# Pooled attention and a gated product: a fourth seven-product unit in the first product, and another order in the second, from tile 3 on

## The chip, the cores and the metric

The kernel runs on one core of a Trainium2 chip. The metric is the device time in microseconds (us) of one execution, from the first instruction to the last output in memory. The chip's engines work side by side, each through its own list of instructions in order, and wait for each other by semaphores: TensorE (PE) multiplies matrices, into the eight banks of PSUM; VectorE (DVE) and ScalarE (ACT) read PSUM and do element-wise work; GpSimd (POOL) adds and starts transfers; SyncE (SP) starts transfers.

## The reference

```python
# q, k, v: batch 8, 8 heads, 576 rows, 64 wide; float32
k_p = k.reshape(B, H, 72, 8, 64).mean(axis=3)      # 576 rows pooled to 72
v_p = v.reshape(B, H, 72, 8, 64).mean(axis=3)
scores = (1 / sqrt(64)) * q @ k_p^T
attn = softmax(scores)
x = (attn @ v_p) as 4608 tokens x 512

h = x @ w_in                     # 512 x 2048, the "first product"
g = h * sigmoid(h)               # SiLU
out = g @ w_out                  # 2048 x 512, the "second product"
```

The 4608 tokens are worked through in nine tiles of 512 (t = 0 to 8). The attention of batch t + 1 runs in the gaps of tile t, so it lies beside tiles 0 to 6 as a whole batch's work and is absent from tiles 7 and 8.

## The kernel before: the parts concerned

A 2 x 2 block product can be had from seven block products in place of eight, at the price of sums of blocks (Strassen's scheme). The kernel uses it in both products, with the products numbered 1 to 7.

In the first product, one **unit** covers four of the sixteen groups of 128 hidden columns: a block is 256 tokens by 256 hidden columns by 256 of the 512 inputs. The unit has seven products of four matmuls, each 256 columns wide. The sums on the weights (`w_sum1`) are made once, those on x (`x_sum`) once a tile. Three units (A, B, C) cover groups 4 to 15, and groups 0 to 3 are computed plainly, each with four matmuls of 512 columns.

```python
UNITS = ((4, 6), (8, 10), (12, 14))

def product(y, n, bank, first):          # product n of unit y
    ...
    for u in range(2):
        next(step)                       # other work is slipped in by count of steps
        for kk in range(2):
            nc.tensor.matmul(ps[y, bank][:, u, :], lhsT=w[:, kk, 128*u : 128*(u+1)],
                             rhs=x[:, kk, :], start=..., stop=kk == 1)

def stage(y, n):
    if n == "2":   product(y, 2, "P", True);  nc.scalar.copy(r_sb, ps[y, "P"])
    elif n == "5": product(y, 5, "Q", True);  tt(out=rr_sb, in0=ps[y, "Q"], in1=r_sb, op=add)
    elif n == "1": product(y, 1, "R", True);  tt(out=t_sb, in0=ps[y, "R"], in1=rr_sb, op=sub)
    elif n == "4": product(y, 4, "P", False); hidden(y, 1, 0, ps[y, "P"])   # SiLU on ScalarE
    elif n == "3": product(y, 3, "Q", False); hidden(y, 0, 1, ps[y, "Q"])
    elif n == "7": product(y, 7, "P", False); tt(out=c_sb[0], in0=ps[y, "P"], in1=t_sb, op=add)
    elif n == "6": product(y, 6, "Q", False); tt(out=c_sb[1], in0=ps[y, "Q"], in1=t_sb, op=add)
    elif n == "h": hidden(y, 0, 0, c_sb[0])
    else:          hidden(y, 1, 1, c_sb[1])

def plain(t, step, g, n0, n):            # one group without the scheme
    for kk in range(4): nc.tensor.matmul(hp_ps[...], lhsT=w_in_sb[:, kk, g*128:(g+1)*128],
                                         rhs=xT[:, kk, ...])        # 512 columns
    nc.scalar.activation(h_T[:, g, ...], hp_ps, func=AF.Silu)
```

P and Q of the units rotate through five PSUM buffers tagged "at", which the attention's tiles use too; R, the plain groups and the three banks of the second product rotate through three tagged "mm". `r_sb`, `rr_sb`, `t_sb` and the two `c_sb` exist once.

In the second product a tile is one such block product, with seven products of sixteen matmuls, 256 columns wide. Its left sides are sums of hidden values (`h_sum`, bf16 operations on VectorE), except for products 3 and 4, which read the plain hidden values `h_T`:

```python
def down_quarters(t, fillers, last=False):
    product(2, KA, KQ); product(5, KA, KQ); product(2, 0, KA)
    nc.scalar.copy(r_sb, ps["P"])
    product(5, 0, KA)
    tt(out=rr_sb, in0=ps["Q"], in1=r_sb, op=add)
    for cc in ((0,), (1,)) if last else ((0, 1),):
        product(1, ...);  tt(out=t_sb, in0=ps["R"], in1=rr_sb, op=sub)
        product(4, ...);  nc.scalar.copy(o_sb[1][:, cs, LO], ps["P"])
        product(3, ...);  nc.vector.tensor_copy(out=o_sb[0][:, cs, HI], in_=ps["Q"])
        product(7, ...);  tt(out=o_sb[0][:, cs, LO], in0=ps["P"], in1=t_sb, op=add); store(...)
        product(6, ...);  tt(out=o_sb[1][:, cs, HI], in0=ps["Q"], in1=t_sb, op=add); store(...)
```

The attention of the next batch and the sums are slipped in between the matmuls at counted steps:

```python
f_down.append((33, lambda: hidden_sum(7, 0, 8)))
...
sc_at, den_at, nu_at = (1, 31, 75), (31, 56, 97), (56, 97, 101)   # scores, denominators, numerators
...
for n in (4, 1, 3, 7, 6):
    f_down.append((98 if t < B - 1 else 44, lambda n=n: unit_x_sum(t + 1, n)))
```

Of the kernel before, what the change touches and what calls it, by code (L numbers as in the profile page):

```python
# [27 lines left out]
FP32 = mybir.dt.float32  # L28
# [8 lines left out]
def kernel(  # L37
# [9 lines left out]
    nc = tc.nc  # L47
# [43 lines left out]
    def ps_tile(shape, dtype, tag, name):  # L91
        return psum.tile(shape, dtype, tag=tag, bufs=banks[tag], name=name)
# [24 lines left out]
            singles.tile([128, 5, 2, 256], BF16, name=f"w_sum1{n}") for n in range(2)  # L117
        )
    ]
    x_sum = singles.tile([128, 5, 2, NQ], BF16, name="x_sum")  # L120
    gate = singles.tile([128, 1], BF16, name="gate")
    c_sb = [singles.tile([128, 2, NQ], FP32, name=f"c_sb{n}") for n in range(2)]
# [54 lines left out]
    def load_one(b, name):  # L177
        st = batches.setdefault(b, {})
        raw = raw_tile(f"{name}_raw", H)
        nc.gpsimd.dma_start(out=raw, in_=source(b, name)[:, :, :PH])  # L180
        st[f"{name}_raw"] = raw
# [10 lines left out]
        )  # L192
        nc.gpsimd.tensor_add(out=dst, in0=raw[:, :, :D], in1=raw[:, :, D : 2 * D])

    def behind_x_sums():
        nc.gpsimd.tensor_copy(out=gate[:1], in_=x_sum[:1, U_XI[6], 0, :1])  # L196

    def pool_k(b):
        pool_rows(kp[:SP], batches[b]["k_raw"])
# [119 lines left out]
    def third(n):  # L319
        return tuple((g, n * QV, (n + 1) * QV) for g in range(2))  # L320
# [78 lines left out]
    def attn_tables():  # L399
        nc.scalar.preload_act_table_set("natural_log_exp_and_others")  # L400
# [13 lines left out]

    UNITS = ((4, 6), (8, 10), (12, 14))
    UW = [
        {
            (i, j): w_in_sb[:, 2 * j : 2 * j + 2, 128 * u : 128 * (u + 2)]  # L420
# [14 lines left out]
    def unit_weight_sum(y, n):  # L435
        a, b = U_W[n]
        nc.vector.tensor_tensor(
            out=w_sum1[y][U_WI[n]], in0=UW[y][a], in1=UW[y][b],
            op=ALU.subtract if n in (6, 7) else ALU.add,
        )  # L440
# [19 lines left out]
    def up(t, fillers, items):  # L460
        step = spread(
            fillers,
            sum(
                KF if len(it) == 3 else 2 * len(it[1].strip("hs")) for it in items
            ),
        )
        ps = {}

        def product(y, n, bank, first):
            if first:  # L470
                tag = "mm" if bank == "R" else "at"
                ps[y, bank] = ps_tile([128, 2, NQ], FP32, tag, f"u_ps{bank}")
            w, x = unit_weights(y, n), unit_x(t, n)
            for u in range(2):
                next(step)
                for kk in range(2):
                    nc.tensor.matmul(  # L477
                        ps[y, bank][:, u, :], lhsT=w[:, kk, 128 * u : 128 * (u + 1)],
                        rhs=x[:, kk, :], start=first and u == 0 and kk == 0,
                        stop=kk == 1, skip_group_check=True,  # L480
                    )

        def hidden(y, i, j, src):
            g = UNITS[y][i]
            nc.scalar.activation(  # L485
                h_T[:, g : g + 2, j * NQ : (j + 1) * NQ], src, func=AF.Silu
            )

        tt = nc.vector.tensor_tensor

        def stage(y, n):
            if n == "2":
                product(y, 2, "P", True)
                nc.scalar.copy(r_sb, ps[y, "P"])  # L494
            elif n == "5":
                product(y, 5, "Q", True)
                tt(out=rr_sb, in0=ps[y, "Q"], in1=r_sb, op=ALU.add)  # L497
            elif n == "1":
                product(y, 1, "R", True)
                tt(out=t_sb, in0=ps[y, "R"], in1=rr_sb, op=ALU.subtract)  # L500
            elif n == "4":
                product(y, 4, "P", False)
                hidden(y, 1, 0, ps[y, "P"])
            elif n == "3":
                product(y, 3, "Q", False)
                hidden(y, 0, 1, ps[y, "Q"])
            elif n == "7":
                product(y, 7, "P", False)
                tt(out=c_sb[0], in0=ps[y, "P"], in1=t_sb, op=ALU.add)  # L509
            elif n == "6":  # L510
                product(y, 6, "Q", False)
                tt(out=c_sb[1], in0=ps[y, "Q"], in1=t_sb, op=ALU.add)  # L512
            elif n == "h":
                hidden(y, 0, 0, c_sb[0])
            else:
                hidden(y, 1, 1, c_sb[1])

        for it in items:
            if len(it) == 3:
                plain(t, step, *it)  # L520
            else:
                for n in it[1]:
                    stage(it[0], n)
        for _ in step:
            pass

    def plain(t, step, g, n0, n):
        tag = "at" if (t, g, n0) == (0, 3, 0) else "mm"
        hp_ps = ps_tile([128, 512], FP32, tag, "hp_ps")
        c0 = (t * NTT + n0) % NX  # L530

        for r0, r1 in ((0, min(n, NX - c0)), (min(n, NX - c0), n)):
            for kk in range(KF) if r1 > r0 else ():
                if r0 == 0:
                    next(step)
                x0 = (c0 + r0) % NX
                nc.tensor.matmul(  # L537
                    hp_ps[:, r0:r1],
                    lhsT=w_in_sb[:, kk, g * 128 : (g + 1) * 128],
                    rhs=xT[:, kk, x0 : x0 + r1 - r0],  # L540
                    start=(kk == 0), stop=(kk == KF - 1),
                )
        nc.scalar.activation(h_T[:, g, n0 : n0 + n], hp_ps[:, :n], func=AF.Silu)  # L543
# [58 lines left out]
    def hidden_sum(n, k0, k1):  # L602
        a, b, op = H_SUMS[n]
        ks = slice(k0, k1)
        nc.vector.tensor_tensor(  # L605
            out=h_sum[n][:, ks, :], in0=quarter(*a, ks), in1=quarter(*b, ks), op=op
        )
# [17 lines left out]
    def left(n, kt, c):  # L625
        cs = slice(128 * c, 128 * (c + 1))
        if n in h_sum:
            return h_sum[n][:, kt, cs]
        i = n - 3
        return h_T[:, i * KQ + kt, i * NQ + 128 * c : i * NQ + 128 * (c + 1)]  # L630
# [55 lines left out]
            pass  # L686


    warm_ps = ps_tile([128, 512], FP32, "mm", "warm_ps")

    def warm_up(n):
# [97 lines left out]
        " C6 Ch Cs g2 g3",  # L789
    )  # L790
    visits = [third(n) for n in range(3)]
    for t in range(NT):
        a = t + 1
        f_up, f_down = [], []
        if t == 0:
            GA = 11
            items = [(g, 0, HS) for g in range(GA)]
            items += [(g, HS, NTT - HS) for g in range(GA)]
            items += [(g, 0, NTT) for g in range(GA, KG)]
            f_up += [(1, lambda: denominators(0, part(0, 1), on_dve=True))]  # L800
            f_up += [(5, lambda: denominators(0, part(1, 1), on_dve=True))]
            f_up += [(13, lambda: numerators(0, part(0, 1)))]
            f_up += [(17, lambda: numerators(0, part(1, 1)))]
        else:
            G = lambda *gs: [(g, 0, NTT) for g in gs]
            if t == 1:
                items = (
                    G(12, 13, 14, 15) + [(0, "25143"), (1, "2"), (0, "7"), (1, "5")]
                    + [(0, "6h"), (1, "1")] + G(0) + [(1, "4"), (0, "s"), (1, "3")] + G(1)
                    + [(1, "7h6")] + G(2) + [(1, "s")] + G(3)  # L810
                )
            else:
                items = []
                for it in THREE[t // B].split():
                    items += [(("BCA".index(it[0])), it[1])] if it[0] in "ABC" else G(int(it[1]))
            if t == 1:
                for n in U_X:
                    f_up.append((0, lambda n=n: unit_x_sum(t, n)))
            for n in (2, 5):
                h_at = 50 if t == B else 54 if t > 1 else 45  # L820
                f_up.append((h_at, lambda n=n: hidden_sum(n, 4, 8)))
            f_up.append((56, lambda: hidden_sum(6, 4, 8)))
            for n, k0 in ((2, 0), (5, 0), (1, 4), (1, 0)):
                f_up.append((64, lambda n=n, k0=k0: hidden_sum(n, k0, k0 + 4)))
            f_down.append((33, lambda: hidden_sum(7, 0, 8)))
            f_down.append((71 if t < B else 50, lambda: hidden_sum(6, 0, 4)))

        for n, t0, f_to, at, parts in (
# [71 lines left out]
        if t == 1:  # L900
            def unit_weight_tiles():
                k_w = big.tile([128, 4, 2, 256], BF16, tag="k_raw2", name="w_sum12")
                v_w = big.tile([128, 4, 2, 256], BF16, tag="v_raw2", name="w_sum12")
                w_sum1.append([k_w[:, i] for i in range(4)] + [v_w[:, 0]])

            f_down.append((72, unit_weight_tiles))
            for i, n in enumerate(U_W):
                f_down.append((73 if i < 2 else 81, lambda n=n: unit_weight_sum(2, n)))
        if t != 1:
            moe_tables()  # L910
        if t == 0:
# [34 lines left out]
```

The softmax here doesn't subtract the row's maximum and nothing guards it: scores larger than these inputs give would overflow.

## Time and profile before

| | |
|---|---|
| time, median of three | 280.02 us (279.89 to 280.05) |
| span of the profiled execution | 278.3 us |
| granted TensorE clock | 1.000 |
| tile 1 (50.8 to 81.0) | 30 us |
| tiles 2, 3, 4, 5, with a batch's attention | 28.7 us each |
| tile 6, with one visit of numerators more | 29.3 us |
| tile 7, without attention | 24.9 us |

The busy share of an engine is the time in which it executed anything, over the span. Matmuls are pipelined, so a busy TensorE can still hold small waits; the sum of its pieces, from the chain of waits, shows whether it does. The attention's matmuls are small ones that use a part of TensorE's array each, four at once.

### The profile page before, as it was taken

To read this page: it belongs to the slowest core of one execution; us is meant where nothing else is said; L and a number is where in the kernel's file an instruction comes from. 1 tells how busy PE (TensorE), PEld (TensorE's weight loads), DVE (VectorE), ACT (ScalarE), POOL (GpSimd) and SP (SyncE) were. 2 spreads that over 40 slices of the span, in tenths; PEclk is the share of its full clock that TensorE was granted. 3 is DMA by queue.
4 is the path that set the end of the run, shared out by engine and by line. 5 is a ranking of instruction groups with operands and counts; after the bars stand their busy time and mean duration, and the time that the engine had idled before them with its cause. 6 is when DMAs were issued, how large, how long until landed. Compare 5 with 4: busy or idle time off the path is not lost.

```text
span 278.3 us, 7160 instructions
## 1 busy us (share of the span) xinstructions
PE 273.8 (98%) x2877; PEld 204.1 (73%) x2877; DVE 220.8 (79%) x415; ACT 189.3 (68%) x369; POOL 98.5 (35%) x104
## 2 busy tenths in 40 slices
PE   8999999999999999999999999999999999999995
PEld 4448444576778677867888788687877778788784
DVE  4886877788998976897689768986888588966982
ACT  1688767468577966797679757985799578326810
POOL 8745217332148430953086107970640000000001
PEclk9999999999999999999999999999999999999999
DMA  7999999896569879569756835599610041005004
GB/s 209 288 259 240 207 326 182 237 200 109 127 86 212 213 104 174 137 162 138 137 109 176 130 65 133 136 132 138 144 44 2 2 104 49 0 11 138 8 0 152
DMA packets 31314, 37.71 MB, mean 135 GB/s; under 512 B 10353, under 2 KB 22257, under 8 KB 31281
## 3 DMA queue, kind: packets, MB, share of 16 engines
q0 software_dynamic: 23920, 27.03, 51.8%
q1 hardware_dynamic: 6928, 9.58, 12.5%
q10 hardware_dynamic: 432, 0.66, 0.6%
q8 instruction: 22, 0.36, 0.5%
q14 instruction: 12, 0.09, 0.1%
HBM read 36.70 MB, written 9.44 MB: 166 GB/s over the span
## 4 chain that ended last, share of the span: by engine, by line
PE 92%; DVE 3%; ACT 3%; issue 1%
PE o_psQ L645 15%; PE hp_ps L537 15%; PE o_psP L645 15%; PE u_psP L477 11%; PE u_psQ L477 11%; PE o_ps L572 5%; PE o_psR L645 5%; PE sc_ps L340 4%; PE u_psR L477 4%; PE nu_ps L384 3%; PE warm_ps L693 3%; PE den_ps L358 2%; DVE h_sum L605 1%; ACT h_T L543 1%; PE warm_ps L697 1%
## 5 line engine op out<-in xcount | busy, mean ns | idle before, releaser
L645 PEld LDWEIGHTS <-h_sum 128*128 128x128 bf16 x640 | 60.7, 98 | 11.5 <-DVE h_sum L605 1.3
L477 PEld LDWEIGHTS <-w_sum 128*128 128x128 bf16 x460 | 45.0, 98 | 8.1 <-issue 0.2
L605 DVE TENSOR_TENSOR h_sum<-h_T 128x1024 bf16<-128x1024 bf16 (+1 forms) x72 | 49.7, 743 | 1.6 <-ACT h_T L543 1.0
L537 PE MATMUL hp_ps<-xT,w_in_sb 128*128 128x512 bf16 (+3 forms) x268 | 50.3, 332 | 0.0
L348 ACT ACTIVATE es<-sc_ps 72x384 bf16<-72x384 f32 (+1 forms) x100 | 39.1, 470 | 8.5 <-PE sc_ps L340 8.3
L543 ACT ACTIVATE h_T<-hp_ps 128x512 bf16<-128x512 f32 (+2 forms) x63 | 31.7, 520 | 10.0 <-PE hp_ps L537 9.2
L537 PEld LDWEIGHTS <-w_in_sb 128*128 128x128 bf16 x268 | 25.6, 98 | 15.1 <-issue 0.8
L485 ACT ACTIVATE h_T<-c_sb 128x512 bf16<-128x512 f32 x46 | 28.8, 629 | 4.4 <-DVE c_sb L509 3.6
L393 DVE TENSOR_TENSOR xT<-nu_ps,rec 128x384 bf16<-128x384 f32 (+1 forms) x50 | 24.0, 533 | 4.9 <-PE nu_ps L384 4.8
L645 PEld LDWEIGHTS <-h_T 128*128 128x128 bf16 x256 | 24.1, 98 | 4.5 <-issue 0.9
L549 POOL DMA_DIRECT2D out_dram<-o_sb x2 | 1.2, 618 | 67.9 <-issue 67.2
L367 ACT ACTIVATE lnd<-den_ps 128x384 f32<-128x384 f32 (+1 forms) x23 | 11.1, 484 | 19.5 <-PE den_ps L358 19.5
L190 POOL TENSOR_TENSOR raw<-raw 72x1024 f32<-72x1024 f32 x10 | 23.6, 2363 | 0.1
L500 DVE TENSOR_TENSOR t_sb<-u_psR,rr_sb 128x512 f32<-128x512 f32 x23 | 15.9, 692 | 6.7 <-PE u_psR L477 5.0
L494 ACT COPY r_sb<-u_psP 128x512 f32<-128x512 f32 x23 | 13.4, 585 | 10.7 <-PE u_psP L477 8.0
L477 PEld LDWEIGHTS <-w_in_sb 128*128 128x128 bf16 x184 | 17.6, 98 | 2.4
L497 DVE TENSOR_TENSOR rr_sb<-u_psQ,r_sb 128x512 f32<-128x512 f32 x23 | 15.7, 682 | 4.0 <-ACT r_sb L494 2.1
L645 PE MATMUL o_psP<-w_out_sb,h_sum 128*128 128x256 bf16 x128 | 17.6, 273 | 0.0
L512 DVE TENSOR_TENSOR c_sb<-u_psQ,t_sb 128x512 f32<-128x512 f32 x23 | 15.8, 687 | 2.3 <-PE u_psQ L477 2.1
L509 DVE TENSOR_TENSOR c_sb<-u_psP,t_sb 128x512 f32<-128x512 f32 x23 | 15.8, 685 | 1.8 <-PE u_psP L477 0.9
L196 POOL COPY gate<-x_sum 1x1 bf16<-1x1 bf16 x5 | 0.9, 181 | 44.7 <-DVE x_sum L444 44.7
L645 PE MATMUL o_psQ<-w_sum,h_sum 128*128 128x256 bf16 x128 | 16.7, 273 | 0.0
(83 smaller groups left out, 528.2 us busy)
## 6 DMA issues: line engine op xcount, KB each, us to landing
out_dram<-o_sb SPq DMA_DIRECT2D x128, 64.0 KB, 1.7
raw<-in_k_dram POOLq DMA_DIRECT2D x10, 576.0 KB, 8.1
raw<-in_v_dram POOLq DMA_DIRECT2D x10, 576.0 KB, 7.6
q_bf<-in_q_dram POOLq DMA_DIRECT2D x6, 576.0 KB, 10.4
w_in_sb<-in_moe_w_in_dram POOLq DMA_DIRECT2D x8, 256.0 KB, 8.6
w_out_sb<-in_moe_w_out_dram POOLq DMA_DIRECT2D x4, 512.0 KB, 13.2
raw<-in_v_dram POOLq DMA_DIRECT2D x2, 768.0 KB, 10.9
raw<-in_k_dram POOLq DMA_DIRECT2D x1, 768.0 KB, 10.8
```

What stands on the lines that cost most here:

```text
L190: nc.gpsimd.tensor_add(out=raw[:, :, : 2 * D], in0=raw[:, :, : 2 * D], in1=raw[:, :, 2 * D :])
L348: nc.scalar.activation(es[:, s, :], sc[s], func=AF.Exp, scale=score_scale)
L393: nc.vector.tensor_mul(out=xT[:, 2 * g0 + c : 2 * (g0 + ng - 1) + c + 1 : 2, cols], in0=nu[c][:, :w].rearrange("r (g n) -> r g n", g=ng), ...
L477: nc.tensor.matmul(ps[y, bank][:, u, :], lhsT=w[:, kk, 128 * u : 128 * (u + 1)], rhs=x[:, kk, :], start=first and u == 0 and kk == 0, stop ...
L485: nc.scalar.activation(h_T[:, g : g + 2, j * NQ : (j + 1) * NQ], src, func=AF.Silu)
L500: tt(out=t_sb, in0=ps[y, "R"], in1=rr_sb, op=ALU.subtract)
L509: tt(out=c_sb[0], in0=ps[y, "P"], in1=t_sb, op=ALU.add)
L512: tt(out=c_sb[1], in0=ps[y, "Q"], in1=t_sb, op=ALU.add)
L537: nc.tensor.matmul(hp_ps[:, r0:r1], lhsT=w_in_sb[:, kk, g * 128 : (g + 1) * 128], rhs=xT[:, kk, x0 : x0 + r1 - r0], start=(kk == 0), stop= ...
L543: nc.scalar.activation(h_T[:, g, n0 : n0 + n], hp_ps[:, :n], func=AF.Silu)
L605: nc.vector.tensor_tensor(out=h_sum[n][:, ks, :], in0=quarter(*a, ks), in1=quarter(*b, ks), op=op)
L645: nc.tensor.matmul(ps[b][:, c, :], lhsT=left(n, kt, c), rhs=W_OUT[n][:, kt, :], start=b not in begun, stop=kt == k1 - 1, skip_group_check= ...
```

## The change

From tile 3 on a new routine `run` takes the place of `up` and `down_quarters`. It does three things:

- Groups 0 to 3 become a fourth unit, E. The sums of its weights are made in tile 2, in what is left of two buffers of k and v and a new tile `w_e`.
- The second product begins with products 4 and 3, which need no sums of hidden values. In the old order the first value copied and added (`r_sb`, `rr_sb`) is M2 and then M2 + M5; in the new order it is M4 and then M4 + M3. Since M2 + M5 is what has to be taken from M1, two operations subtract the finished quarters M4 + M2 and M3 + M5, which ScalarE has copied to `o_sb`, and t = M1 + (M4 + M3) - (M4 + M2) - (M3 + M5).
- The order of all work in a tile, attention too, is written out as a list of tokens (`PROGRAM`). C2 is product 2 of unit C (a and s are its SiLUs of `c_sb`); h2h is the high half of hidden sum 2, h2l the low; d40 is the first fourth of product 4 of the second product; u1 and u2 are the two subtractions; sc, de and nu are scores, denominators and numerators of a visit, npp the numerators left over from the batch before; q, k are transposes; x sums of x for the next tile; o the last addition; T1 and T2 switch ScalarE's tables.

Two smaller parts: in tile 1 the hidden sum of product 7 moves from step 33 to 44, and the copy of product 5's quarter goes from VectorE to ScalarE in `run`.

```diff
-    UNITS = ((4, 6), (8, 10), (12, 14))
+    UNITS = ((4, 6), (8, 10), (12, 14), (0, 2))
...
+    def down_stages(t, last):
+        bank = {2: "P", 5: "Q", 1: "R", 4: "P", 3: "Q", 7: "P", 6: "Q"}
...
+        def after(n, cc=(0, 1), tail=False):
+            if n == 4:
+                nc.scalar.copy(r_sb, ps["P"])
+            elif n == 3:
+                tt(out=rr_sb, in0=ps["Q"], in1=r_sb, op=add)
+            elif n == 2:
+                nc.scalar.copy(o_sb[1][:, :, LO], ps["P"])
...
+            elif n == 5:
+                nc.scalar.copy(out=o_sb[0][:, :, HI], in_=ps["Q"])
...
+            elif n == 1:
+                tt(out=t_sb[:, cs], in0=ps["R"][:, cs], in1=rr_sb[:, cs], op=add)
+            elif n == 7:
+                tt(out=o_sb[0][:, cs, LO], in0=ps["P"][:, cs], in1=t_sb[:, cs], op=add)
...
+        def part_of(tok):
+            if tok == "o":
+                return after(6)
+            n = int(tok[1])
+            if tok[0] == "u":
+                src = o_sb[1][:, :, LO] if n == 1 else o_sb[0][:, :, HI]
+                nc.vector.tensor_tensor(out=rr_sb, in0=rr_sb, in1=src, op=sub)
+                return
...
+            i = int(tok[2])
+            k0 = 2 * i if n == 4 else 2 * (i ^ 2)
+            matmuls(n, k0, k0 + 2)
...
+    PROGRAM = (
+        "C2 C5 B2 q0 C1 C4 B5 C3 A2 q1 B4 C7 Ca C6 B1 B3 A5 B7 Cs E2 B6 A1 Ba A3 E5 Bs "
+        "A4 q2 E4 k q3 A6 E3 A7 Aa As E1 h7h E7 E6 d40 npp Ea d41 Es h2h d42 d43 h5h T1 "
+        "h2l d30 d31 d32 d33 sc0 h1l d20 d21 h6l d22 h5l d23 sc1 de0 h1h d50 d51 d52 "
+        "h6h d53 d10 d11 h7l u1 sc2 de1 d12 u2 d13 d70 nu0 d71 de2 nu1 T2 d72 d73 d60 "
+        "x4 x3 d61 x6 d62 x1 d63 o x7 "
+    )
...
+    T4 = 3
     for t in range(NT):
         a = t + 1
+        if t >= T4:
+            run(t)
+            continue
...
-            f_down.append((33, lambda: hidden_sum(7, 0, 8)))
+            f_down.append((33 if t > 1 else 44, lambda: hidden_sum(7, 0, 8)))
...
+                w_sum1.append([v_w[:, 1 + i] for i in range(3)] + [w_e[:, i] for i in range(2)])
...
+        if t == 2:
+            for i, n in enumerate(U_W):
+                f_down.append((76 + 2 * i, lambda n=n: unit_weight_sum(3, n)))
```

In the last tile, what follows product 5 runs for one half of the tokens and then the other (products 1, 7 and 6 each), as products 1, 4, 3, 7 and 6 did before.

More of the change, by code (lines that the diff above doesn't have):

```diff
@@ L119 @@
     ]
+    w_e = singles.tile([128, 2, 2, 256], BF16, name="w_sum1e")
     x_sum = singles.tile([128, 5, 2, NQ], BF16, name="x_sum")
@@ L193, in pool_rows, with behind_x_sums @@
         nc.gpsimd.tensor_add(out=dst, in0=raw[:, :, :D], in1=raw[:, :, D : 2 * D])
-    def behind_x_sums():
-        nc.gpsimd.tensor_copy(out=gate[:1], in_=x_sum[:1, U_XI[6], 0, :1])
+    def behind_x_sums(n=6):
+        nc.gpsimd.tensor_copy(out=gate[:1], in_=x_sum[:1, U_XI[n], 0, :1])
     def pool_k(b):
@@ L466, in up, with unit_stages @@
         )
+        stage = unit_stages(t, step)
+        for it in items:
+            if len(it) == 3:
+                plain(t, step, *it)
+            else:
+                for n in it[1]:
+                    stage(it[0], n)
+        for _ in step:
+            pass
+    def unit_stages(t, step):
         ps = {}
@@ L516, in stage @@
                 hidden(y, 1, 1, c_sb[1])
[L518 to L525, printed above, removed]
+        return stage
     def plain(t, step, g, n0, n):
@@ L686, in down_quarters, with matmuls, columns @@
             pass
+    def down_stages(t, last):
+        ps = {}
+        bank = {2: "P", 5: "Q", 1: "R", 4: "P", 3: "Q", 7: "P", 6: "Q"}
+        begun = set()
+        add, sub = ALU.add, ALU.subtract
+        tt = nc.vector.tensor_tensor
+        def matmuls(n, k0, k1, cs=(0, 1)):
+            b = bank[n]
+            for kt in range(k0, k1):
+                for c in cs:
+                    nc.tensor.matmul(
+                        ps[b][:, c, :], lhsT=left(n, kt, c), rhs=W_OUT[n][:, kt, :],
+                        start=b not in begun,
+                        stop=kt == k1 - 1, skip_group_check=True,
+                    )
+                    begun.add(b)
+        def after(n, cc=(0, 1), tail=False):
+            cs = slice(cc[0], cc[-1] + 1)
+            if n == 4:
[4 more added lines that the diff above has]
+                nc.scalar.copy(o_sb[1][:, :, LO], ps["P"])
+                if last:
+                    store(t, 3, LO, (nc.gpsimd,))
+            elif n == 5:
+                nc.scalar.copy(out=o_sb[0][:, :, HI], in_=ps["Q"])
+                if last:
+                    store(t, 1, HI)
+            elif n == 1:
+                tt(out=t_sb[:, cs], in0=ps["R"][:, cs], in1=rr_sb[:, cs], op=add)
+            elif n == 7:
+                tt(out=o_sb[0][:, cs, LO], in0=ps["P"][:, cs], in1=t_sb[:, cs], op=add)
+                for c in cc:
+                    store(t, c, LO if tail else FULL, (nc.scalar if tail else nc.sync,))
+            else:
+                tt(out=o_sb[1][:, cs, HI], in0=ps["Q"][:, cs], in1=t_sb[:, cs], op=add)
+                for c in cc:
+                    if tail:
+                        store(t, 3, HI, both)
+                    else:
+                        store(t, 2 + c, FULL, (nc.gpsimd if last else nc.sync,))
+        def part_of(tok):
[6 more added lines that the diff above has]
+                return
+            if not ps:
+                for b in "PQR":
+                    ps[b] = ps_tile([128, 2, CQ], FP32, "mm", f"o_ps{b}")
+            i = int(tok[2])
+            k0 = 2 * i if n == 4 else 2 * (i ^ 2)
+            matmuls(n, k0, k0 + 2)
+            if i == 3 and n != 6:
+                after(n)
+        def columns(c):
+            for n in (1, 7, 6):
+                matmuls(n, 0, KQ, (c,))
+                after(n, (c,), c == 1)
+        return part_of, columns
@@ new lines, with run @@
+    PROGRAM = (
[5 rows of a table added]
+    )
+    def run(t):
+        a = t + 1
+        attn, last = a < B, t == NT - 1
+        stage = unit_stages(t, iter(int, 1))
+        part_of, columns = down_stages(t, last)
+        toks = PROGRAM.split()
+        gate_on = int([x for x in toks if x[0] == "x"][-1][1])
+        attn_toks = ("T1 T2 k npp q0 q1 q2 q3 sc0 sc1 sc2 de0 de1 de2 nu0 nu1").split()
+        if last:
+            i = toks.index("d10")
+            sums = [x for x in toks[i:] if x[0] in "hu"]
+            toks = toks[:i] + sums + ["L0", "L1"]
+        toks = [x for x in toks if attn or x not in attn_toks]
+        if a == B - 1:
+            toks.insert(1 + max(toks.index("de2"), toks.index("nu1"), toks.index("o")), "nu2")
+        if t == T4:
+            toks.insert(0, "T2")
+        if attn:
+            if a + 1 < B - 1:
+                load_q(a + 1)
+            behind_x_sums(6 if t == T4 else gate_on)
+            pool_k(a)
+            if a + 1 < B:
+                load_one(a + 1, "k")
+            pool_v(a)
+            if a + 1 < B:
+                load_one(a + 1, "v")
+                if a + 1 == B - 1:
+                    load_q(a + 1)
+                load_rest(a + 1, "k")
+                load_rest(a + 1, "v")
+        for x in toks:
+            if x[0] in "ABCE" and x[1] in "2514376as":
+                stage("ABCE".index(x[0]), {"a": "h"}.get(x[1], x[1]))
+            elif x[0] == "L":
+                columns(int(x[1]))
+            elif x[:2] == "de":
+                denominators(a, visits[int(x[2])])
+            elif x[0] in "dou":
+                part_of(x)
+            elif x[0] == "h":
+                k0 = 4 if x[2] == "h" else 0
+                hidden_sum(int(x[1]), k0, k0 + 4)
+            elif x == "T1":
+                attn_tables()
+            elif x == "T2":
+                moe_tables()
+            elif x == "k":
+                k_transpose(a)
+            elif x == "npp":
+                numerators(a - 1, visits[2])
+            elif x[0] == "q":
+                n = int(x[1])
+                q_transpose(a, n % 2, n // 2)
+            elif x[:2] == "sc":
+                scores(a, visits[int(x[2])])
+            elif x[:2] == "nu":
+                numerators(a, visits[int(x[2])])
+            elif not last:
+                unit_x_sum(t + 1, int(x[1]))
```

## The prediction

> **What bounds the kernel now.** I read the page's busy shares first. TensorE is at 98%, and its row of slices is full from the second slice on, so a gain has to come out of TensorE's own work unless another engine is pushed over the edge.
>
> ```profile
> PE 273.8 (98%) x2877; PEld 204.1 (73%) x2877; DVE 220.8 (79%) x415; ACT 189.3 (68%) x369; POOL 98.5 (35%) x104
> PE   8999999999999999999999999999999999999995
> DVE  4886877788998976897689768986888588966982
> ```
>
> "Busy" may hide waits, so next the stretches, one for each tile (columns: PE, weight loads, VectorE, ScalarE and GpSimd busy, then clock and DMA). Tiles 2 to 5 take 28.7 us each, tile 6 29.3, tile 7, which has no attention beside it, 24.9.
>
> ```profile
> 168.20:196.90 28.70, 28.70 (x327) 22.61 (x325) 23.28 (x42) 22.08 (x43) 17.33 (x17) 1.00 0.95 140
> 226.20:251.10 24.90, 24.90 (x215) 20.65 (x213) 20.21 (x34) 12.91 (x23) 0.00 (x0) 1.00 0.14 36
> ```
>
> The reader is to see VectorE at 23.28 of 28.7 us, 81%: it has 5.4 us to spare in such a tile, ScalarE 6.6. Then the chain of waits inside tile 5 (start, length, what) shows what TensorE does with its time.
>
> ```profile
> 177.18 0.86 PE hp_ps L537 x4
> 178.04 0.44 PE u_psQ L477 x4
> 178.48 1.73 PE hp_ps L537 x8
> 180.21 0.22 PE o_psP L645 x2
> 180.43 0.47 PE sc_ps L340 x16
> 180.89 0.76 PE o_psP L645 x6
> 181.65 0.87 PE o_psQ L645 x8
> ```
>
> Four 512-column matmuls take 0.86 us (0.216 each), eight 256-column ones 0.87 (0.109), and each piece starts where the last ended. I add a tile up: 16 plain matmuls x 0.216 = 3.45; 21 unit products x 4 x 0.109 = 9.2; the second product, 112 x 0.109 = 12.2; attention 3.4 (three scores at 0.47, denominators and numerators together 1.83, the transposed k 0.13). That is 28.2. The other 0.5 is five times about 0.1 us at the entry to the small attention matmuls: in the timeline two 0.11 us matmuls stand in 0.32 us (180.04 to 180.36) before the scores. So TensorE waits for nothing in tiles 2 to 8, and also not at the join of the first and second product, which the new order is built to bridge.
>
> **What the Trainium skill says.** "TensorE: Matmul & The Clock Gate", Back-to-back issue gap, gives N/2.4 + 2.5 ns for a warm matmul: 109 ns at 256 columns, 216 at 512, which is what this trace shows; the section's lower sustained figure at 512 columns is not seen here. "VectorE: DVE Perf Modes", The perf-mode tier table, says tensor_tensor runs at one element a cycle with float32 or PSUM operands and at two in bf16 from SBUF. The trace agrees: 692 ns for 512 float32 elements from PSUM, 684 for 1024 bf16 ones. The same page, The DRAIN you can't avoid, says a next op waits until the pipe is empty. The trace agrees only in part: seven hidden sums of 684 ns take 4.29 us, 0.61 each, so independent ones overlap; where an op needs the one before it (t_sb at 176.84, the c_sb that adds it at 177.66) the step is 0.82.
>
> **The change part by part.**
>
> First, *plain groups to a unit* (tiles 3 to 8). Removed: 16 x 0.216 = 3.45 us of TensorE. Added: 28 x 0.109 = 3.06. That is 0.39 us a tile on the bound, x6 = **-2.34 us**.
>
> Second, *order of attention*. The numerators of the third visit now stand alone behind the first part of product 4, and the first visit's alone behind the first part of product 7. Entries go from five to six a tile, about 0.1 us each, in the four attention tiles 3 to 6: **+0.4 us**.
>
> Third, *VectorE*. A unit adds four 128x512 float32 ops (at 0.61 a step, 2.44 us), the mending two subtractions (1.22, an estimate from the same row), the hidden sum of product 7 in halves 0.07; the copy of o_sb that goes to ScalarE takes away 0.61. So 23.28 + 3.1 = 26.4 of 28.4 us, 93%. ScalarE: one r_sb copy (0.59) and four SiLUs (0.60 to 0.63) for four plain ones (0.59), with the o_sb copy: about +1.3, so 23.4. Neither passes TensorE in total; the question is order. I walk one attention tile by hand, with time 0 at its first product. VectorE starts the first rr_sb at about 1.3. Through its queue to the last c_sb there are sixteen unit ops, four transposes and one hidden sum: at 0.61 for independent neighbours, 0.82 for dependent ones and 0.4 for a transpose that makes 13.2 us, so the numerators' two multiplications start at about 14.5 and the sums h2 (high), h5 (high), h2 (low) end at about 16.1, 16.7 and 17.4. TensorE ends its 28 products at about 12.3; products 4 and 3 of the second product read plain h, which ScalarE has ready, and with the numerators and the first scores they last until 16.9. Then come h2 high, ready, and h2 low at 17.8, ready by 0.2 or short by as much once each hand-over (0.2 us in the timeline) is counted. h5 low, h1 high and h6 high follow with as little margin. I put 0.15 us of waits on each of the four attention tiles, a choice: **+0.6 us**. In tiles 7 and 8 VectorE has no transposes and no multiplications, TensorE 24.5 us of work and VectorE some 23: **+0**.
>
> Fourth, *the weights of the fourth unit*. Five sums of 0.35 us in tile 2 (five x_sums of the same shape take 1.76), set at steps 76 to 84. There VectorE sits idle 1.0 and 1.1 us ahead of two o_sb operations, so they fit: **0**.
>
> Fifth, *tile 1's seventh hidden sum*, moved from step 33 to 44. Now that 1.21 us operation at 71.46 stands in front of the pooled v's copies at 72.59, and TensorE's numerators wait for those: denominators and sixteen numerators take from 72.74 to 73.75, 1.01 us, where 165.14 to 165.75, 0.61 us, is normal. Moved, most of 0.4 returns: **-0.35 us**.
>
> Sixth, *the end*. The last matmul is still followed by one half-width VectorE op (0.42) and a store; nothing is moved there.
>
> Sum: -2.34 + 0.4 + 0.6 + 0 - 0.35 = -1.7, so 280.0 - 1.7 = 278.3 us.
>
> **The rivals.** *No new wait at all*: the order was chosen so that margins hold, and I overstate the steps. Then -2.34 - 0.35 + 0.4 = -2.3, 277.7; if entries cost nothing more, 277.3. For it: every early operand of the second product is now plain h. Against it: VectorE at 93% in order. *VectorE takes over as bound* in tiles 3 to 6: its queue is in order, r_sb, rr_sb and t_sb exist once and are passed between units, so each of the sixteen unit ops can hold up the next product, and the end of a tile (two multiplications, t_sb, o_sb, five x_sums) runs into the next one's start. With dependent steps at 0.82 for half of its unit ops VectorE comes to about 27.5, and two or three hand-overs of 0.2 us and waits on TensorE make a period near 29: +0.3 on each of four tiles against today, less 0.8 for tiles 7 and 8 and 0.35 for tile 1: 280.0. For it: the walk's margins of 0.2. Against it: the 26.4 by overlapped steps. *PSUM buffers*: five rotating "at" banks now serve eight unit tiles, then keys, numerators and scores. The third unit's Q needs the first one's P read; in my walk it is by 0.4 us. A miss would cost a few tenths a tile, as in the second rival. *The join pays more*, if the present trace hid waits there: then under 277; the added-up tile speaks against it.
>
> **Range and chances.** The firm terms are 0.39 a tile and tile 1's 0.35; the soft one is waits, 0 to 0.5 us a tile in four tiles. Without them 277.3 to 277.7, with the second rival 280.0. I give 277.1 to 280.0 eight times in ten. Two per cent is 5.6 us: a gain of that size exceeds all that TensorE is relieved of, a loss needs over 1 us of new wait in every changed tile. Faster by over 2% 0.01, within 0.97, slower 0.02.
>
> **What would show it.** In the changed profile: attention tiles of 28.4 to 28.6 us (not 28.7 or more), tiles 7 and 8 at 24.5; no hp_ps matmul after tile 2; VectorE near 26.4 in a tile; the numerators of tile 1 back at 0.6; waits of weight loads on h_sum of 0.1 to 0.3 a tile. If weight loads or products wait for rr_sb or c_sb for over 0.5 us a tile, the second rival holds. The prediction is wrong if the tiles stay at 28.7 or more with TensorE showing gaps, or fall under 28.2.

## The result, and the profile after

The changed kernel takes 281.26 us (median of six, 281.08 to 281.56) against 280.10 for the kernel before: 1.0037 times as long, 95% interval 1.0023 to 1.0051. It is slower, by about 1 us, where 1.7 us less was predicted, and lies over the upper end of the stated range, 280.0.

The page's busy shares and VectorE's row of slices:

```profile
PE 273.0 (98%) x2923; PEld 208.9 (75%) x2933; DVE 240.2 (86%) x455; ACT 193.6 (69%) x379; POOL 98.4 (35%) x104
...
DVE  4886877788999979999889978997999788987894
```

VectorE has 19.4 us more to do and is at nine tenths or more in many slices from tile 3 on. TensorE has 0.8 us less busy time in a span that is 1.1 us longer. By stretches of a tile's length, one from 1.1 us into tile 5 and one from 1.1 us into tile 7 (columns as before):

```profile
168.20:197.10 28.90, 28.82 (x338) 23.68 (x336) 26.24 (x48) 23.03 (x45) 17.30 (x17) 1.00 1.00 142
...
226.60:251.80 25.20, 24.76 (x227) 21.79 (x225) 22.37 (x39) 12.57 (x24) 0.00 (x0) 1.00 0.16 40
```

VectorE's 26.24 us in an attention tile is what was predicted (26.4). But TensorE is no longer busy for the whole of the stretch. A table by tile, from the first product of each tile to the first of the next (and to the end of the span for tile 8):

| tile | before, us | after, us | difference |
|---|---|---|---|
| up to tile 2's end | 109.78 | 109.29 | -0.49 |
| 3 | 28.73 | 28.90 | +0.17 |
| 4 | 28.78 | 28.92 | +0.14 |
| 5 | 28.73 | 28.90 | +0.17 |
| 6 | 29.29 | 29.45 | +0.16 |
| 7 | 24.87 | 25.24 | +0.37 |
| 8 and the end | 28.14 | 28.72 | +0.58 |

Tile 1 gained (29.80 us after, 30.21 before; the other 0.08 us of the first row lies ahead of it), the tiles with a fourth unit all lost. Where, is seen in the chain of waits within tile 5:

```profile
174.69 0.45 PE u_psR L489 x4
175.14 0.02 issue
175.17 0.69 DVE c_sb L524
175.86 0.03 issue
175.89 0.02 DVEq L512
175.91 0.04 issue
175.95 0.70 DVE t_sb L512
176.66 0.03 issue
176.68 0.05 DVEq L509
176.73 0.04 issue
176.78 0.70 DVE rr_sb L509
177.48 0.04 issue
177.52 0.60 PE u_psQ L489 x4
```

Before, this chain stayed on TensorE through the whole tile. Now it leaves it for 2.3 us: the last c_sb of unit B, t_sb of unit A and rr_sb of unit E follow one another on VectorE, and only then may product 3 of unit E be added to Q. "DVEq" is VectorE's own sequencer holding the next operation. The steps are 0.78 and 0.83 us, for operations of 0.69. TensorE's previous product began at 176.84 and took 0.44, so it stands still for 0.24 us. In tiles 7 and 8 the same wait is 0.37 us, in tile 7 from 235.52 (235.08 + 0.44) to 235.89:

```profile
235.08 0.60 PE L489 MATMUL u_psQ<-x_sum,w_sum 128*128 128x256 bf16 x4
235.89 0.60 PE L489 MATMUL u_psQ<-x_sum,w_in_sb 128*128 128x256 bf16 x4 [0.21 <-DVE rr_sb L509]
```

VectorE's row of eight operations from the first c_sb of unit C to rr_sb of E takes the same 5.04 us in tile 5 (171.74 to 176.78) and in tile 7 (230.11 to 235.15). TensorE reaches product 3 of E 0.13 us sooner in tile 7, since the transposed k, which takes 0.13, is not there.

The lone numerators, in TensorE's timeline of tile 5:

```profile
179.70 0.60 PE L705 MATMUL o_psP<-w_sum,h_T 128*128 128x256 bf16 x4
180.23 0.51 PE L385 MATMUL nu_ps<-es,vp 72*32 72x192 bf16 x16
180.68 1.48 PE L705 MATMUL o_psP<-w_sum,h_T 128*128 128x256 bf16 x12
```

Four matmuls from 179.70 need 0.44 us, and the next large one begins at 180.68: the sixteen numerators cost 0.54 us. The first visit's numerators, at 191.78, cost 0.54 too. Behind denominators sixteen take 0.33, as the chain within tile 5 of the kernel before shows for 32:

```profile
187.85 0.28 PE den_ps L358 x4
188.13 0.66 PE nu_ps L384 x32
```

In tile 7 the second product has a wait of its own (VectorE, then TensorE):

```profile
242.03 0.69 DVE L717 TENSOR_TENSOR rr_sb<-o_psQ,r_sb 128x512 f32<-128x512 f32 x1
242.63 3.70 DVE L610 TENSOR_TENSOR h_sum<-h_T 128x1024 bf16<-128x1024 bf16 x6
```

```profile
243.31 1.04 PE L705 MATMUL o_psQ<-w_out_sb,h_sum 128*128 128x256 bf16 x8
244.58 1.05 PE L705 MATMUL o_psQ<-w_out_sb,h_sum 128*128 128x256 bf16 x8 [0.23 <-DVE h_sum L610]
```

The low half of hidden sum 5 is the third of six sums, so it is done at 242.63 + 3 x 0.61 = 244.5; product 5 was ready for it at 243.31 + 0.87 = 244.18. It waits 0.40 us, in tile 8 the same.

So there are three suspects: the hand-overs of the single buffers rr_sb and t_sb, the lone numerators, and the order of the hidden sums. The rival to all three is that VectorE has too much work in total, in which case a wait that is removed comes back at the next product.

### The profile page after: what moved, and what is told of

Read it like the earlier page. It is cut to its first block, busy times and chain, and to the rows that moved or that the text cites. A ratio compares the mean times of both kernels' runs of the same rounds, so it can differ in the third digit from the quotient of the medians.

```text
span 279.4 us, 7356 instructions
## 1 busy us (share of the span) xinstructions
PE 273.0 (98%) x2923; PEld 208.9 (75%) x2933; DVE 240.2 (86%) x455; ACT 193.6 (69%) x379; POOL 98.4 (35%) x104
## 4 chain that ended last, share of the span: by engine, by line
PE 87%; DVE 9%; issue 2%; ACT 1%; DVEq 0%
PE u_psP L489 12%; PE u_psQ L489 11%; PE o_psQ L705 10%; PE o_psP L705 9%; PE hp_ps L542 8%; PE o_ps L577 5%; PE u_psR L489 5%; PE sc_ps L341 4%; PE o_psR L705 4%; PE o_psQ L650 4%; PE o_psP L650 4%; PE nu_ps L385 3%; PE warm_ps L837 3%; PE den_ps L359 2%; DVE h_sum L610 2%; DVE t_sb L512 2%
## 5 line engine op out<-in xcount | busy, mean ns | idle before, releaser
L489 PEld LDWEIGHTS <-w_sum 128*128 128x128 bf16 x532 | 51.7, 98 | 7.1 <-issue 0.3
L705 PEld LDWEIGHTS <-h_sum 128*128 128x128 bf16 x480 | 45.1, 98 | 9.5 <-issue 2.2
L497 ACT ACTIVATE h_T<-c_sb 128x512 bf16<-128x512 f32 x58 | 35.6, 626 | 13.3 <-DVE c_sb L521 13.1
L542 PE MATMUL hp_ps<-xT,w_in_sb 128*128 128x512 bf16 (+2 forms) x151 | 25.9, 318 | 0.3
L489 PEld LDWEIGHTS <-w_in_sb 128*128 128x128 bf16 x232 | 22.5, 98 | 4.6 <-issue 1.8
L548 ACT ACTIVATE h_T<-hp_ps 128x512 bf16<-128x512 f32 (+2 forms) x39 | 18.1, 476 | 5.8 <-PE hp_ps L542 4.8
L542 PEld LDWEIGHTS <-w_in_sb 128*128 128x128 bf16 x156 | 14.6, 98 | 8.5 <-issue 0.7
L705 PEld LDWEIGHTS <-h_T 128*128 128x128 bf16 x192 | 18.4, 98 | 2.7 <-issue 0.6
L489 PE MATMUL u_psQ<-x_sum,w_in_sb 128*128 128x256 bf16 x116 | 17.5, 272 | 0.7 <-DVE rr_sb L509 0.4
L497 ACT ACTIVATE h_T<-u_psQ 128x512 bf16<-128x512 f32 x29 | 17.1, 590 | 1.0 <-PE u_psQ L489 0.7
L497 ACT ACTIVATE h_T<-u_psP 128x512 bf16<-128x512 f32 x29 | 16.7, 598 | 1.2 <-PE u_psP L489 1.1
```

What stands on the lines that cost most here:

```text
L489: nc.tensor.matmul(ps[y, bank][:, u, :], lhsT=w[:, kk, 128 * u : 128 * (u + 1)], rhs=x[:, kk, :], start=first and u == 0 and kk == 0, stop ...
L497: nc.scalar.activation(h_T[:, g : g + 2, j * NQ : (j + 1) * NQ], src, func=AF.Silu)
L542: nc.tensor.matmul(hp_ps[:, r0:r1], lhsT=w_in_sb[:, kk, g * 128 : (g + 1) * 128], rhs=xT[:, kk, x0 : x0 + r1 - r0], start=(kk == 0), stop= ...
L705: nc.tensor.matmul(ps[b][:, c, :], lhsT=left(n, kt, c), rhs=W_OUT[n][:, kt, :], start=b not in begun, stop=kt == k1 - 1, skip_group_check= ...
```

## The experiments

Times are medians; each ratio is to the kernel before, measured on the same chip, with its 95% interval in brackets.

**A second rr_sb and t_sb.**

```diff
+        rr_u, t_u = [rr_sb, rr_sb], [t_sb, t_sb]
+        if t >= 3:
+            rr_u[1], t_u[1] = (...)   # float32 views of the two halves of h_sum[5], idle in the first product
-                tt(out=rr_sb, in0=ps[y, "Q"], in1=r_sb, op=ALU.add)
+                tt(out=rr_u[y % 2], in0=ps[y, "Q"], in1=r_sb, op=ALU.add)
# and likewise t_u[y % 2] for t_sb in products 1, 7 and 6
```

> The changed kernel, with a second rr_sb and a second t_sb for every other unit (they lie in the hidden sum of product 5, which is idle then). Theory of the hand-over: product 3 of unit E waits 0.24 us in tiles 3 to 6 and 0.37 us in tiles 7 and 8 because the last c_sb of unit B, t_sb of A and rr_sb of E must follow one another on VectorE, each step 0.8 us as they share a buffer; with two of each the steps are 0.6, the wait goes, and the time falls by 4 x 0.24 + 2 x 0.37 = 1.7 us against the changed kernel, to about 0.6 us under the kernel before. Rival, VectorE has too much work in total: the wait only moves to a later product, and the time stays within 0.5 us of the changed kernel.

Measured: 279.32 us, 0.9971 (0.9961 to 0.9982) of the kernel before, 1.9 us under the changed kernel. Tiles 3 to 5 take 28.67 us in place of 28.90. VectorE's timeline of tile 5 (the second buffers bear the name h_sum), with the last c_sb of B, t_sb of A and rr_sb of E:

```profile
174.29 0.69 DVE L530 TENSOR_TENSOR c_sb<-u_psQ,h_sum 128x512 f32<-128x512 f32 x1
...
174.34 0.63 ACT L503 ACTIVATE h_T<-c_sb 128x512 bf16<-128x512 f32 x1
...
174.90 0.68 DVE L518 TENSOR_TENSOR t_sb<-u_psR,rr_sb 128x512 f32<-128x512 f32 x1
...
175.60 0.69 DVE L515 TENSOR_TENSOR h_sum<-u_psQ,r_sb 128x512 f32<-128x512 f32 x1
...
176.33 0.60 PE L495 MATMUL u_psQ<-x_sum,w_sum 128*128 128x256 bf16 x4
...
176.77 0.60 PE L495 MATMUL u_psQ<-x_sum,w_in_sb 128*128 128x256 bf16 x4
```

The steps are 0.61 and 0.70, and product 3 of E (176.77) starts 0.44 us after the product before it: no wait. The same number of VectorE operations, with nothing shared between neighbours, no longer bounds the first product. The rival of total work fails here. The gain is a little over the theory's, since VectorE also reaches the hidden sums sooner: product 5 waits 0.20 us in tiles 7 and 8, where it was 0.40.

**A second rr_sb alone.**

```diff
-            rr_u[1], t_u[1] = (...)
+            rr_u[1], _ = (...)
```

> The changed kernel with a second rr_sb alone, t_sb single. If each shared buffer costs its own 0.2 us step: the wait of unit E's product 3 falls from 0.24 to about 0.03 us in tiles 3 to 6 and from 0.37 to 0.16 in tiles 7 and 8, some 1.2 us less than the changed kernel. If only t_sb matters: no change.

Measured: 279.69 us, 0.9985 (0.9975 to 0.9994), 1.6 us under the changed kernel; tiles 3 to 5 at 28.67, so the wait there is gone as foretold. It is gone in tiles 7 and 8 too, where 0.16 us was to be left. In the timeline rr_sb now follows t_sb by 0.61 us, while t_sb still follows c_sb by 0.78: each shared buffer costs its own step, and rr_sb's is enough for product 3 of unit E. The step of t_sb shows further on: product 5 still waits 0.39 us in tiles 7 and 8, and each takes 0.2 us more than with both doubled (28.35 against 28.16 us in tile 8).

**The changed kernel without the mending.** The two subtractions are left out, so the two quarters that add t_sb lack M4 + M2 and M3 + M5.

```diff
-        "... d11 h7l u1 sc2 de1 d12 u2 d13 ..."
+        "... d11 h7l sc2 de1 d12 d13 ..."
```

> The changed kernel without its two subtractions, so that the quarters with t_sb lack them (part of the computation is left out). What the mending itself costs: by the theory of the hand-over it lies in VectorE's free time and the product 3 of unit E still waits, so tiles 3 to 7 stay as they are and only the last tile loses its 0.17 us wait: 0.1 to 0.2 us less than the changed kernel. By the rival, VectorE's total work: 1.2 us less of it in each of six tiles takes 0.2 us or more off each, over 1.2 us in all.

Measured: 281.14 us, 1.0038 (1.0025 to 1.0050), a tenth under the changed kernel. Tiles 3 to 5 stay at 28.90 to 28.91, and the last loses 0.17 us. Twelve operations fewer on VectorE gain next to nothing: the mending lies in free time. The run does not weigh the load ahead of the two waits, for VectorE stands idle behind the mending's place (1.1 us before t_sb in tile 7) and meets the next tile's products as before.

**The sums in the order of need.**

```diff
-        "... sc0 h1l d20 d21 h6l d22 h5l d23 sc1 de0 h1h d50 ..."
+        "... sc0 h5l d20 d21 h1h d22 h1l d23 sc1 de0 h6l d50 ..."
```

> The changed kernel, with VectorE's hidden sums in the order in which the products need them (h5 low, h1 high, h1 low, h6 low in place of h1 low, h6 low, h5 low, h1 high). Theory: in tiles 7 and 8 product 5 waits 0.40 us for the low half of h5, so 0.8 us less in all than the changed kernel, and tiles 3 to 6 stay at 28.9. Rival, VectorE is simply behind: product 1 or 6 then waits as long, and nothing is gained.

Measured: 280.81 us, 1.0032 (1.0020 to 1.0045), only about half of what was expected. Tiles 6 and 7 together fall from 54.69 to 54.29 us: in tile 7 the wait is gone, and product 5 runs through. In tile 8 it moved, as the rival had it (28.72 us, as in the changed kernel):

```profile
269.83 1.04 PE L705 MATMUL o_psR<-w_sum,h_sum 128*128 128x256 bf16 x8
...
270.03 0.59 ACT L723 COPY o_sb<-o_psQ 128x512 f32<-128x512 f32 x1 [1.16 <-PE o_psQ L705]
...
271.01 1.49 DVE L746 TENSOR_TENSOR rr_sb<-rr_sb,o_sb 128x512 f32<-128x512 f32 x2
...
271.16 1.05 PE L705 MATMUL o_psP<-w_sum,h_sum 128*128 128x256 bf16 x8 [0.29 <-DVE h_sum L610]
```

Product 1 for one half of the tokens (269.83) takes only 0.87 us here, as the last tile works by halves, so the last sum in the list, that of product 7, comes 0.46 us too late. Each theory holds in one tile.

**The numerators in company, both.**

```diff
-        "... E7 E6 d40 npp Ea d41 ... d32 d33 sc0 ... d70 nu0 d71 de2 nu1 ..."
+        "... E7 E6 d40 Ea d41 ... d32 d33 npp sc0 ... d70 d71 nu0 de2 nu1 ..."
```

> The changed kernel, with the leftover numerators moved right in front of the first scores, and the first visit's right in front of the last denominators. Theory of the entries: sixteen numerators that stand alone take 0.54 us of TensorE, in a block with other small matmuls 0.33; so 2 x 0.21 in each of four tiles, 1.7 us less than the changed kernel (0.6 us under the kernel before). Rival, the place does not matter, or the moved numerators make VectorE's products with rec come later and hold up the hidden sums: within 0.5 us of the changed kernel.

Measured: 284.68 us, 1.0165 (1.0151 to 1.0179), 3.4 us over the changed kernel: neither theory foresaw this size. The list of waits names it:

```profile
PE sc_ps L341 <- DVE xT L394: 3.6, 4, 0.9
```

Four times, once in each attention tile, the first scores wait 0.9 us for VectorE's multiplication that reads the numerators. The scores need four of the five "at" buffers, the numerators hold two until VectorE has multiplied them. Next to the scores there is no time for that: the block of numerators and scores takes 2.14 us of TensorE, where the two apart took 0.54 and 0.56. The lone place of the leftover numerators is thus not an oversight: it pays 0.2 us of TensorE to have the buffers free. Attention tiles took 29.71 us.

**The order alone.** Groups 0 to 3 are plain again, the rest as changed.

```diff
-        "... Cs E2 B6 A1 Ba A3 E5 Bs A4 q2 E4 k q3 A6 E3 A7 Aa As E1 h7h E7 E6 d40 npp Ea d41 Es h2h ..."
+        "... Cs g0 B6 A1 Ba A3 g1 Bs A4 q2 k q3 A6 g2 A7 Aa As g3 h7h d40 npp d41 h2h ..."
```

> The changed kernel without its fourth unit: groups 0 to 3 are plain again (four matmuls of 512 columns each), and all else, the new order of the second product with its two subtractions and of the attention, stays. If the new order costs only its two lone numerators (0.32 us in each of four tiles) and VectorE, with three units, holds nothing up: tiles 3 to 6 at 29.05 us, tiles 7 and 8 at 24.9, the whole 0.9 us over the kernel before (1.3 less tile 1's 0.4). If the new order in itself makes VectorE late (two more operations, h5 low behind h1 and h6), tiles 7 and 8 show the 0.4 us wait of product 5 again, and it is 1.7 us over.

Measured: 282.12 us, 1.0065 (1.0052 to 1.0077), 1.8 us over the kernel before. By the number that is the second of the two forecasts; the tiles lie between them. Tiles 3 to 5 take 29.06 to 29.10 us, 0.32 to 0.34 over before; that is the two lone numerators. Tile 7 is 0.32 us longer than before and tile 8, up to its last matmul, 0.53; product 5 waits 0.20 us in each, half of the 0.40, and weight loads wait 0.8 us in all for hidden sums: VectorE's order of sums is late there even with three units. Another 0.36 us of the profiled execution lies behind its last matmul (3.74 us, in the kernel before 3.38), where no theory put it; its cause is not shown.

**The units alone**, with the old order of the second product and of the attention.

```diff
-        if t >= T4:
-            run(t)
-            continue
+    FOUR = ("C2 C5 B2 C1 C4 B5 C3 A2 B4 C7 Ch C6 B1 B3 A5 B7 Cs E2 B6 A1 Bh A3 E5 Bs "
+            "A4 E4 A6 E3 A7 Ah As E1 E7 E6 Eh Es")      # then down_quarters as before
```

> The changed kernel with its four units, but from tile 3 on with the old order of the second product and of the attention (no subtractions; the second product begins with products 2 and 5). If the unit's own hand-overs are the only cost: 0.39 saved and 0.24 to 0.37 lost a tile, so 0.4 to 1 us under the kernel before, with tile 1's 0.4 in it. If the second product has to wait for the sums of E's hidden values, as it was changed to avoid: about 0.5 to 1.5 us of wait at the join in each of six tiles, 3 to 8 us over the kernel before.

Measured: 297.52 us, 1.0632 (1.0604 to 1.0660), 17 us over, twice the upper forecast. TensorE's waits over the span (the wait on the matmul, then on its weight load, the same standstill in part), and the first one of tile 5's in the timeline, with what follows it:

```profile
PE o_psP L650 <- DVE h_sum L610: 13.0, 8, 2.1
```

```profile
PEld L650 <- DVE h_sum L610: 16.9, 14, 2.3
```

```profile
186.08 0.39 PE L650 MATMUL o_psP<-w_out_sb,h_sum 128*128 128x256 bf16 x2 [1.76 <-DVE h_sum L610]
...
187.63 1.92 PE L650 MATMUL o_psQ<-w_out_sb,h_sum 128*128 128x256 bf16 x8
189.33 1.78 PE L650 MATMUL o_psP<-w_out_sb,h_sum 128*128 128x256 bf16 x8
```

```profile
187.60:190.90 3.30, 3.30 (x18) 2.35 (x16) 3.20 (x7) 3.19 (x6) 1.33 (x2) 0.51 2.37 112
```

The second product waits for the hidden sums, which lie behind the last units in VectorE's queue: 1.9 us at the start of the second product in tiles 3 to 7, with 0.3 more further on in tiles 3, 4 and 6 and 0.8 in tile 7, and 1.6 and 2.2 in tile 8. In tile 5 another 1.6 us are no wait: from 187.6 to 190.9 the granted clock is 0.51 (the last figure but two in the row), and fifteen matmuls start 0.21 us apart in place of 0.11; why the clock fell there is not shown. In this form the fourth unit costs far more than it saves, and the changed kernel is about 16 us faster. But the sums and the attention keep the steps that were set for three units; other steps were not tried, so how much of the 16 us needs the new order of the second product stays open.

**Tile 1's sum alone**, in the kernel before.

```diff
-            f_down.append((33, lambda: hidden_sum(7, 0, 8)))
+            f_down.append((33 if t > 1 else 44, lambda: hidden_sum(7, 0, 8)))
```

> The kernel before, with only the hidden sum of product 7 in tile 1 moved from step 33 to 44. Theory: the 0.4 us that the numerators of tile 1 waited are gained for good, 0.14% under the kernel before, and every later tile starts 0.4 to 0.5 us earlier. Rival, the gain is lost again at a later wait: no difference.

Measured: 279.68 us, 0.9980 (0.9973 to 0.9987). The gain stays.

**Both buffers, the order of need, and the last tile's product 7 first.**

```diff
# the doubled rr_sb and t_sb, the sums in the order of need, and for the last tile:
+            toks.remove("h7l")
+            toks.insert(toks.index("h6l"), "h7l")
```

> Two rr_sb and t_sb as in the run before, with the hidden sums in the order of need (h5 low, h1 high, h1 low, h6 low), and in the last tile the sums of product 7 ahead of those of product 6. Theory: the two waits are independent, so that what is left in tiles 7 and 8 behind the doubled buffers (0.2 us at product 5 in each) goes, and the last tile's product 7 does not take the wait over as it did with the reordered sums alone: 0.4 to 0.6 us under the doubled buffers alone, 1.3 us under the kernel before. Rival, VectorE's backlog just shows at the next sum: no difference to the doubled buffers alone.

Measured: 278.95 us, 0.9962 (0.9948 to 0.9976). The medians differ by 0.4 us from the doubled buffers alone (279.32), with intervals that overlap; the tiles show less than forecast: 0.2 us in tiles 6 and 7 (53.68 against 53.89), in tile 8 nothing (28.2 in both). There the wait moved on to product 1 of the second half, which needs t_sb to be out of the bank R:

```profile
271.30 1.03 PE L711 MATMUL o_psR<-w_sum,h_sum 128*128 128x256 bf16 x8 [0.27 <-DVE t_sb L733]
```

That wait is 0.43 us long. VectorE's backlog is real in the last tile, where the rival was right.

**The same, with the first visit's numerators in company.**

```diff
-        "... d70 nu0 d71 de2 nu1 ..."
+        "... d70 d71 nu0 de2 nu1 ..."
```

> The same, and the first visit's numerators moved by four matmuls, right in front of the last denominators; the leftover numerators stay where they are. A lone block of numerators costs 0.54 us of TensorE against 0.33 in company: 0.2 us in each of four tiles, 0.8 us less than without. If their later place holds up VectorE's end of the tile, and with it the first rr_sb of the next one: nothing gained, or lost.

Measured: 277.98 us, 0.9927 (0.9914 to 0.9939): the fastest, 2.1 us under the kernel before and 3.3 under the changed one. Tiles 3 to 5 take 28.45 us, 0.22 less, as expected. TensorE's timeline of tile 5, with the two blocks now beside the denominators:

```profile
190.98 0.51 PE L385 MATMUL nu_ps<-es,vp 72*32 72x192 bf16 x16
...
191.32 0.34 PE L359 MATMUL den_ps<-es,ones 72*32 72x384 bf16 x4
...
191.38 1.95 DVE L394 TENSOR_TENSOR xT<-nu_ps,rec 128x384 bf16<-128x384 f32 x4 [0.47 <-PE nu_ps L385]
...
191.49 0.50 PE L385 MATMUL nu_ps<-es,vp 72*32 72x192 bf16 x16
```

The first numerators take 0.34 us until the denominators start.

## Why the prediction was wrong, point by point

*Plain groups to a unit, -0.39 us a tile*: right. Twenty-eight products stand in 12.24 us, and in the best version a tile takes 28.45 us, which is 28.73 - 0.39 + 0.11.

*Order of attention, +0.4 us*: the term was mis-sized. The entry to the small matmuls was right, 0.09 us for every block in tile 5, and so was one entry more. But numerators that stand alone take 0.54 us, 0.12 more than the entry and the 0.33 that they take behind denominators, and there are two such blocks. That makes 0.09 + 2 x 0.12 = 0.33 us a tile, where the sum over tile 5's pieces has 0.32 (28.90 = 28.73 - 0.39 + 0.24 + 0.32), and the order alone 0.32 to 0.34. Over four tiles that is 1.3 us, not 0.4. That one of the two could be moved was not seen; that the other has to stand alone for its buffers, neither.

*VectorE, 0.15 us a tile in tiles 3 to 6 and 0 in 7 and 8*: this step failed. Its total was right (26.2 for 26.4), and so was the step of 0.82 us between dependent operations. But I used that step to find when the hidden sums are ready, and did not hold rr_sb of E against product 3 of E, where the wait was: 0.24 us in each of tiles 3 to 6, 1.0 us in all in place of 0.6. For tiles 7 and 8 I compared totals, 24.5 with 23, and wrote 0. There product 3 of E waited 0.37 and product 5 for h5 low 0.40, and tile 8 has a further 0.17 at the change of halves; by the table and the 0.39 saved, tile 7 lost 0.76 us and tile 8 0.97. This zero is the largest part of the error. VectorE has fewer transposes and multiplications there, but none of them lay between C's c_sb and E's rr_sb, so that row stays 5.04 us long while TensorE, without attention, comes sooner. Half of product 5's wait is there without the fourth unit too (0.20 us in the order alone).

*The fourth unit's weights, 0*: right; tile 2 takes 28.74 us, where it took 28.73.

*Tile 1, -0.35 us*: right in mechanism, and 0.4 in size. In the changed kernel the denominators and numerators of tile 1 take from 72.64 to 73.25:

```profile
72.64 0.35 PE L359 MATMUL den_ps<-es,ones 72*32 72x384 bf16 x4
72.81 0.50 PE L385 MATMUL nu_ps<-es,vp 72*32 72x192 bf16 x16
73.25 0.94 PE L650 MATMUL o_psP<-w_sum,h_T 128*128 128x256 bf16 x7
```

*The end, 0*: the tail after the last matmul is unchanged, but the last tile's halves are a place where VectorE is behind (0.17 us), which I had not looked for.

*The rivals*: of "VectorE takes over as bound" the mechanism named there, single buffers passed between units so that a unit's operation holds up the next product, is what happened; its size, 280.0, was too low, as it gave tiles 7 and 8 their full gain. The rest of that rival, a VectorE full by total, is refuted for the attention tiles by the doubled buffers. *PSUM buffers* did not bind in the changed kernel, and bound at once when the numerators were moved. *The join*: that the old kernel showed no wait there was right, but said nothing of the new one; with four units and its old steps the old order waits 1.9 us or more there in each of tiles 3 to 7.

The sum with the measured terms: -2.34 (units) + 1.3 (lone numerators) + 1.0 (tiles 3 to 6) + 1.7 (tiles 7 and 8) - 0.5 (up to tile 2's end, 0.4 of it in tile 1) = 1.2, against 1.1 in the spans.

## What to carry to other kernels

A saving on a full TensorE is worth what is left after the hand-overs it adds: write down, for each accumulating product, the operation on another engine that must have read its bank before, and follow that engine's queue to there, also in the stages where the load is light. If neighbours in one engine's queue share a scratch buffer, give every other one its own before judging that the engine is full; space that is idle in that stage will do. A block of work that looks badly placed may hold its place for its buffers, so move one such block at a time.

## What the runs showed of the hardware that was not expected

- Sharing a buffer between two operations of the same engine costs time although they run in order: c_sb to t_sb to rr_sb stepped by 0.78 and 0.83 us with single buffers, by 0.61 and 0.70 with two, for operations of 0.69. "VectorE: DVE Perf Modes", Rules for kernel authors, of the Trainium skill says to minimise the count of operations and not the semaphores; here the count stayed, only what neighbours share changed, and the time fell by 1.9 us, so the measurement decides. The section on the DRAIN of that page, which the prediction quotes, goes on to say that a next operation that is not held starts earlier; the 0.61 us of independent operations fit that. What in the hand-over takes the 0.2 us was not tried apart.
- Going from large matmuls (128 x 128) to small ones cost TensorE 0.09 us at each of the blocks of scores, denominators and numerators in tile 5. Sixteen numerators (72 x 32) alone between large ones take 0.54 us, behind denominators 0.33, so they pay another 0.12; scores alone pay no more than the entry (0.56 = 0.09 + 0.47). Why the two differ is not shown.
